# Loading the next chunk's activations in four parts, spread over two output products, in an attention and feed-forward kernel on one core

## The chip, the core and the metric

One core of one Trainium2 chip. The metric is the device time of one execution in microseconds (us). A kernel is run several times; a comparison uses runs of the two kernels on the same chip.

## The reference, cut to what matters

Hash attention is followed by a feed-forward block with a squared ReLU. The change lies in the second block:

```python
def _moe_ref(x, w_in, w_out):          # x: 3072 x 512, w_in: 512 x 2048, w_out: 2048 x 512
    h = x @ w_in
    r = np.maximum(h, 0.0)
    return ((r * r) @ w_out).astype(np.float32)
```

## The kernel before

Attention writes its result, transposed, to a buffer `x_all` in device memory. The feed-forward block then takes three chunks of 1,024 tokens. For each chunk it makes the hidden layer, and then the output in `project`, as seven output products (numbered 0 to 6) of a Strassen-like scheme. Each product is seven adds into PSUM. The chunk's x has a single buffer, so the next chunk's x is loaded while `project` runs, when x is no longer read.

In chunk 0 alone, `project` also prepares weights for the later chunks. At the start of each of products 0 to 3, `factor_units` loads two pieces of 256 KB ("h"), makes four sums of them on VectorE ("DVE" in the profiles), and stores pieces and sums. Loads of h, stores and loads of x all go through GpSimd's DMA queue. The stationary weights of each add ("leaf", 256 KB) are loaded through ScalarE's queue.

```python
    def load_x(i):
        x = p_c.tile([P, NFT, NCH], FP32, name="x")
        nc.gpsimd.dma_start(out=x, in_=x_all[:, :, i * NCH:(i + 1) * NCH])
        xs[i] = x, [p_c.tile([P, 2, NCH // 2], FP32, name=f"t_x{n}") for n in range(3)]

        def factor_units(n):
            src = [new_h()... for _ in range(2)]
            for j in range(2):
                nc.gpsimd.dma_start(out=src[j], in_=w_in_7[j * NQ + n, :, 5:7])
            sums = [new_h()... for _ in range(2)]
            sums_a(...)                                    # four sums on DVE
            for lo, hi, t in (...):
                nc.gpsimd.dma_start(out=w_in_49[n, :, :, lo:hi], in_=t)

        def product(n, w, at, bt, c11, c12, c21, c22, hook=None):
            ...
            add(0, at(0), bt["11"], True, False)
            one = keep(0, "one")
            add(1, at(1), bt["21"], True, True)
            if hook:
                hook()
            ...                                            # adds 3 to 6
            add(0, at(2), bt["t4"], False, True)           # the seventh reads what hook subtracted

            for k in range(7):
                ...
                if i == 0 and k < NQ:
                    factor_units(k)
                ...
                def hook():
                    y21 = b[:, NQ:NR, 0:QN]
                    minus(y21, y21, t2)
                    if k + 1 < 7 and k not in (1, 3):
                        inner_sums(k + 1)
                    ...
                product(NQ, QN, a_with_load, bt, ..., hook)
                if k == 0 and i + 1 < NCHUNK:
                    load_x(i + 1)
                if k in (3, 4) and i + 1 < NCHUNK:
                    sum_x(i + 1, 2 * k - 5)                # the first readers of the new x
                    sum_x(i + 1, 2 * k - 4)
```

On DVE the order within a product is: weight sums of `factor_units`, the hook's subtraction, inner sums of the next product, then sums of the outputs.

## Time and profile before

| | before |
|---|---|
| median of 3 runs | 880.21 us (880.0 to 881.27) |
| profiled run | 879.66 us, span 877.9 us |
| TensorE (PE) busy | 864.8 us |
| DVE busy | 760.4 us |
| TensorE idle in the output stage of chunk 0 (427 to 513 us) | 0.72 us |
| TensorE idle in the output stage of chunk 1 (605 to 692 us) | 0.00 us |

How to read it: one engine is busy for 98.5% of the span, so a change that moves no arithmetic is judged by the few places where that engine idles. The lines themselves are in the prediction below. In a timeline row the columns are start, duration, engine, source line, operation, output and input tiles, number of instructions, and in brackets the idle time just before, with what ended it ("issue": the profile shows nothing that the engine waited for).

### The profile page before, as it was taken

To read this page: it belongs to the slowest core of one execution; us is meant where nothing else is said; L and a number is where in the kernel's file an instruction comes from. 1 tells how busy PE (TensorE), PEld (TensorE's weight loads), DVE (VectorE), ACT (ScalarE), POOL (GpSimd) and SP (SyncE) were. 2 spreads that over 40 slices of the span, in tenths; PEclk is the share of its full clock that TensorE was granted. 3 is DMA by queue.
4 is the path that set the end of the run, shared out by engine and by line. 5 is a ranking of instruction groups with operands and counts; after the bars stand their busy time and mean duration, and the time that the engine had idled before them with its cause. 6 is when DMAs were issued, how large, how long until landed. Compare 5 with 4: busy or idle time off the path is not lost.

```text
span 877.9 us, 12130 instructions
## 1 busy us (share of the span) xinstructions
PE 864.8 (99%) x4340; PEld 518.7 (59%) x4340; DVE 760.4 (87%) x1099; ACT 391.5 (45%) x673; POOL 107.0 (12%) x172
## 2 busy tenths in 40 slices
PE   8999999999999999999999999999999999999996
PEld 3444444444444444444688865556888755568885
DVE  5999999999999998888779968888889788888875
ACT  6988888888888852222211123332111233321110
POOL 2000000000000001554231011111000211110002
PEclk9999999999999999999999999999999999999998
DMA  9777967998788536999897764536756754355565
GB/s 176 142 149 134 233 153 156 188 253 225 179 176 225 156 105 213 299 267 283 292 353 239 181 160 168 173 118 222 285 151 187 167 165 155 124 167 154 158 175 105
DMA packets 224131, 167.09 MB, mean 190 GB/s; under 512 B 164448, under 2 KB 181344, under 8 KB 224064
## 3 DMA queue, kind: packets, MB, share of 16 engines
q1 hardware_dynamic: 189152, 87.19, 41.0%
q0 software_dynamic: 12528, 41.30, 15.2%
q10 hardware_dynamic: 22384, 37.76, 14.0%
q8 instruction: 36, 0.59, 0.3%
q14 instruction: 31, 0.25, 0.1%
HBM read 124.52 MB, written 41.68 MB: 189 GB/s over the span
## 4 chain that ended last, share of the span: by engine, by line
PE 95%; DVE 2%; ACT 1%; DMA 1%; issue 0%; ACTq 0%; DVEq 0%
PE acc L712 40%; PE st L396 17%; PE acc L931 16%; PE xo L438 14%; PE acc L884 6%; PE hash L346 2%; PE tot L455 1%; DVE total L428 1%; DMA k_nat<-in_k_dram 1%; ACT bits L356 1%; ACT e L413 0%; PE xo L477 0%; DVE x_t L493 0%; PE tp L309 0%; DVE recs L487 0%
## 5 line engine op out<-in xcount | busy, mean ns | idle before, releaser
L413 ACT ACTIVATE e<-st 128x1024 f32<-128x1024 f32 x192 | 145.1, 810 | 44.9 <-PE st L396 41.0
L396 PE MATMUL st<-feat,feat 64*128 64x512 f32 (+1 forms) x768 | 150.4, 483 | 0.0
L438 PE MATMUL xo<-e,v_nat 128*64 128x512 f32 (+1 forms) x768 | 134.8, 492 | 0.0
L712 PE MATMUL acc<-b,leaf 128*128 128x256 f32 x600 | 133.2, 379 | 0.7 <-issue 0.7
L712 PEld LDWEIGHTS acc<-b,leaf 128*128 128x128 f32 x600 | 113.8, 190 | 17.1 <-issue 1.7
L428 DVE TENSOR_TENSOR total<-total,e 128x1536 f32<-128x1536 f32 x64 | 112.4, 1757 | 8.2 <-ACT e L413 3.6
L438 PEld LDWEIGHTS xo<-e,v_nat 128*64 128x64 f32 x768 | 51.3, 136 | 82.2 <-issue 74.3
L931 PE MATMUL acc<-t_x,w_unit 128*128 128x512 f32 x192 | 90.2, 592 | 0.0
L396 PEld LDWEIGHTS st<-feat,feat 64*128 64x128 f32 x768 | 66.0, 188 | 33.0 <-issue 23.2
L712 PE MATMUL acc<-t,leaf 128*128 128x256 f32 x336 | 76.3, 380 | 0.0
L356 ACT ACTIVATE bits<-hash,lifts 32x384 bf16<-32x384 f32 x120 | 68.6, 572 | 2.3 <-PE hash L346 0.5
L712 PEld LDWEIGHTS acc<-t,leaf 128*128 128x128 f32 x336 | 63.6, 190 | 9.4 <-DVE t L516 0.5
L796 DVE SCALAR_TENSOR_TENSOR b<-h 128x512 f32<-128x512 f32 x96 | 65.7, 691 | 3.0
L396 PE MATMUL st<-bits,bits 64*128 64x256 bf16 (+1 forms) x384 | 63.1, 325 | 1.7 <-ACT e L413 1.2
L931 PE MATMUL acc<-x,w_unit 128*128 128x512 f32 x128 | 60.1, 592 | 0.0
L712 PE MATMUL acc<-x,w_unit 128*128 128x512 f32 x128 | 56.6, 594 | 0.0
L712 PE MATMUL acc<-b_t,leaf 128*128 128x256 f32 x240 | 53.8, 379 | 0.0
L931 PEld LDWEIGHTS acc<-t_x,w_unit 128*128 128x128 f32 x192 | 36.5, 190 | 28.9 <-issue 26.8
L719 ACT COPY two<-acc 128x256 f32<-128x256 f32 (+1 forms) x29 | 12.5, 431 | 87.9 <-PE acc L712 63.1
L719 ACT COPY one<-acc 128x256 f32<-128x256 f32 (+1 forms) x29 | 12.5, 431 | 85.1 <-PE acc L712 46.9
L712 PEld LDWEIGHTS acc<-b_t,leaf 128*128 128x128 f32 x240 | 45.5, 190 | 6.2
L396 PEld LDWEIGHTS <-bits 64*128 64x128 bf16 x384 | 23.5, 93 | 42.5 <-issue 38.4
(159 smaller groups left out, 1165.5 us busy)
## 6 DMA issues: line engine op xcount, KB each, us to landing
leaf<-w_out ACTq DMA_DIRECT2D x142, 256.0 KB, 3.1
w_unit<-w_in SPq DMA_DIRECT2D x16, 640.0 KB, 4.0
raw<-in_moe_w_in_dram SPq DMA_DIRECT2D x16, 512.0 KB, 5.6
raw<-in_moe_w_out_dram SPq DMA_DIRECT2D x16, 512.0 KB, 4.6
w_unit<-w_in SPq DMA_DIRECT2D x8, 896.0 KB, 8.1
w_out<-sums POOLq DMA_DIRECT2D x16, 448.0 KB, 6.8
sum<-w_in SPq DMA_DIRECT2D x16, 448.0 KB, 4.8
v_nat<-in_v_dram SPq DMA_DIRECT2D x16, 384.0 KB, 4.3
```

The source lines that it names most:

```text
L346: nc.tensor.matmul(out=banks[g * NR_B:(g + 1) * NR_B, h, 0:HS], lhsT=projs[rows], rhs=feat[pr, w][rows, c * HS:(c + 1) * HS], start=True, ...
L356: nc.scalar.activation(out=t[h * D:h * D + NR_B, c * HS:(c + 1) * HS], in_=hashed[pr, w][at, h, 0:HS], func=ACTF.Sign, scale=HUGE, bias=li ...
L396: nc.tensor.matmul(out=st[:, h, 0:hi - lo], lhsT=src[pr, 1][rows, key], rhs=src[pr, 0][rows, lo:hi], start=first, stop=not first,)
L413: nc.scalar.activation(out=e[:, :, lo:hi], in_=sts[i][:, :, 0:hi - lo], func=ACTF.Exp, scale=scale)
L428: nc.vector.tensor_tensor(out=totals[pr], in0=totals[pr], in1=weights[pr, kt][:, :, 0:S], op=ALU.add)
L438: nc.tensor.matmul(out=xo[h * D:(h + 1) * D, lo:hi], lhsT=nat[pr, "v_nat"][:, h, kt * D:(kt + 1) * D], rhs=weights[pr, kt][:, h, lo:hi], s ...
L455: nc.tensor.matmul(out=tot[g * 32:(g + 1) * 32, 0:HS], lhsT=ones, rhs=totals[pr][:, h, c * HS:(c + 1) * HS], start=True, stop=True,)
L712: nc.tensor.matmul(out=acc[to], lhsT=a(i), rhs=b(i), start=first and i == 0, stop=last and i == n - 1, skip_group_check=True,)
L719: nc.scalar.copy(out=t, in_=acc[of])
L796: nc.vector.scalar_tensor_tensor(out=out, in0=h, scalar=0.0, in1=h, op0=ALU.max, op1=ALU.mult)
L884: nc.tensor.matmul(out=out, lhsT=w[:, a], rhs=b, start=start, stop=stop, skip_group_check=True)
L931: nc.tensor.matmul(out=acc[to], lhsT=w[:, PLACE[a], f], rhs=bt[b](f), start=first and f == 0, stop=last and f == NFT // 2 - 1, skip_group_ ...
```

## The change

Its intent is to thin out the burst of the 2,048 KB load: four parts of 512 KB, two during and after output product 0, two during and after product 1.

```diff
-    def load_x(i):
-        x = p_c.tile([P, NFT, NCH], FP32, name="x")
-        nc.gpsimd.dma_start(out=x, in_=x_all[:, :, i * NCH:(i + 1) * NCH])
-        xs[i] = x, [...]
+    def load_x(i, n=slice(0, NFT)):
+        if i not in xs:
+            x = p_c.tile([P, NFT, NCH], FP32, name="x")
+            xs[i] = x, [...]
+        nc.gpsimd.dma_start(out=xs[i][0][:, n], in_=x_all[:, n, i * NCH:(i + 1) * NCH])
...
                     minus(y21, y21, t2)
+                    if k < 2 and more:
+                        load_x(i + 1, slice(2 * k, 2 * k + 1))
...
-                if k == 0 and i + 1 < NCHUNK:
-                    load_x(i + 1)
+                if k < 2 and i + 1 < NCHUNK:
+                    load_x(i + 1, slice(2 * k + 1, 2 * k + 2))
```

More of the change, by code (lines that the diff above doesn't have):

```diff
@@ L549 @@
     xs = {}
-    def load_x(i):
-        x = p_c.tile([P, NFT, NCH], FP32, name="x")
-        nc.gpsimd.dma_start(out=x, in_=x_all[:, :, i * NCH:(i + 1) * NCH])
-        xs[i] = x, [p_c.tile([P, 2, NCH // 2], FP32, name=f"t_x{n}") for n in range(3)]
+    def load_x(i, n=slice(0, NFT)):
+        if i not in xs:
+            x = p_c.tile([P, NFT, NCH], FP32, name="x")
+            xs[i] = x, [p_c.tile([P, 2, NCH // 2], FP32, name=f"t_x{n}") for n in range(3)]
+        nc.gpsimd.dma_start(out=xs[i][0][:, n], in_=x_all[:, n, i * NCH:(i + 1) * NCH])
     w_unit = {}
```

## The prediction

> **What bounds the kernel now.** I read the page first: busy shares, then the chain that ended last.
>
> ```profile
> PE 864.8 (99%) x4340; PEld 518.7 (59%) x4340; DVE 760.4 (87%) x1099; ACT 391.5 (45%) x673; POOL 107.0 (12%) x172
> ...
> PE 95%; DVE 2%; ACT 1%; DMA 1%; issue 0%; ACTq 0%; DVEq 0%
> ```
>
> TensorE is busy for 864.8 of 877.9 us and carries 95% of the chain. The change moves no arithmetic, so it can gain only where TensorE stands still for the moved load, and lose only where the load newly makes it stand still. Next, busy time by stage. The load of the next chunk's x is issued in the output stage of chunk 0 (427 to 513 us) and of chunk 1 (605 to 692 us).
>
> ```profile
> 427.00:513.00 86.00, 85.28 (x393) 74.24 (x392) 79.26 (x123) 11.75 (x31) 19.34 (x30) 1.00 0.82 254
> ...
> 605.00:692.00 87.00, 87.00 (x400) 75.59 (x399) 78.66 (x116) 12.02 (x32) 8.05 (x13) 1.00 0.68 203
> ```
>
> Columns: stretch, its length, then busy us (and count) of PE, weight loads, DVE, ACT, POOL, then granted clock, DMA share, GB/s. TensorE loses 0.72 us in the first stage and nothing in the second. Thus the most that the change can win is 0.72 us, 0.08%. DVE is busy 79.26 of 86 us, so it has little room to be late.
>
> The timeline tells where the 0.72 us come from. First GpSimd's issues:
>
> ```profile
> 434.25 0.95 POOL L554 DMA_DIRECT2D x<-x_all  x1
> 435.01 1.28 POOL L837 DMA_DIRECT2D h<-w_in  x2
> 447.36 0.68 POOL L846 DMA_DIRECT2D w_in<-h  x1 [11.07 <-DMA h<-w_in]
> ```
>
> The 2,048 KB of x go out at 434.25 (11.9 us to landing, so 446.2), and the two 256 KB weight pieces h, issued right after, land only at 447.4 and 448.4: they queue behind x. Then all engines:
>
> ```profile
> 448.12 0.43 DVE L510 TENSOR_TENSOR h<-h 128x256 f32<-128x256 f32 x1 [1.21 <-DMA h<-w_in]
> ...
> 449.59 1.22 DVE L516 TENSOR_TENSOR b<-b,t 128x1024 f32<-128x1024 f32 x1
> ...
> 450.91 1.97 PE L712 MATMUL acc<-b,leaf 128*128 128x256 f32 x8 [0.72 <-issue]
> ...
> 456.54 0.42 DVE L510 TENSOR_TENSOR h<-h 128x256 f32<-128x256 f32 x1 [3.02 <-DMA h<-w_in]
> ...
> 473.41 1.22 DVE L516 TENSOR_TENSOR b<-b,t 128x1024 f32<-128x1024 f32 x1
> ```
>
> DVE waits 1.21 us for h, makes the four weight sums, then the subtraction of 449.59 that ends at 450.81. The seventh add of output product 1 reads that result and starts at 450.91, after 0.72 us of idling. The page labels the wait "issue"; I put it down to this subtraction, since the instruction order has TensorE wait for DVE there and the times fit. The last two rows are the same pair for product 2's weights and product 3's subtraction; they matter below.
>
> **What the Trainium skill says.** "DMA: Bandwidth & Descriptors", section "Queues, rings and completion order": each DMA engine consumes one queue's descriptors in ring order and round-robins between queues by packet. The trace agrees: h lands 1.2 us after x, and while x runs, the leaf weights of another queue take 7.1 to 7.9 us instead of the median 3.1. Section "Anatomy of one DMA — SWDGE (gpsimd) path": about 2.0 us plus bytes over 436 GB/s, so 512 KB alone would be an estimated 3.2 us and 2,048 KB 6.8 us; the trace has 11.9 us for the latter, because the DMA share is 0.97 to 1.04 from 436 to 452 us. The same section says that waits are held by the issuing sequencer and not by the DMA engines. "Perfetto Trace Analysis", section "Tensor Engine Instruction (MATMUL, LD_WEIGHTS)" has the elementwise engines as strict FIFO: the DVE wait for h delays everything after it, as the rows above show.
>
> **The change part by part.**
>
> (a) Count and bytes: two loads of 2,048 KB become eight of 512 KB, the same bytes and 4 KB rows. GpSimd gains six issues at an estimated 0.55 us (its 192 KB issues take 0.54), 3.3 us on an engine 12% busy: nothing on the path. DVE, TensorE and ScalarE keep their order.
>
> (b) Chunk 1 to 2. The order has no other GpSimd issue between the four parts, and all four stand where the old one stood, after the last peak loads (614.56 us). They go back to back and the stage keeps its zero idle: 0.0 us.
>
> (c) Chunk 0 to 1, first half. The order on GpSimd's queue becomes: stores of product 0's weight sums, x parts 0 and 1, h loads for product 1, its four stores, x parts 2 and 3, h loads for product 2. With x moving at (2,048 KB in 11.9 - 2.0 us) about 0.21 MB/us, 1 MB is 5 us: h for product 1 lands at an estimated 434.25 + 2 + 5 + 2 = 443.3 instead of 448.4. DVE reaches those sums at 446.9 (448.12 less 1.21) and no longer waits. The subtraction ends 1.2 us sooner, TensorE does not stop: **-0.72 us**, all of the idle.
>
> (d) Chunk 0 to 1, second half. Now x parts 2 and 3 stand before the h loads for product 2. DVE makes product 1's sums 1.2 us earlier, so the sum stores go out at about 448.2 instead of 449.5. From there the queue has 0.52 MB of stores, 1.05 of x and 0.52 of h. Before, the stores and h alone landed at 456.4, 7 us after 449.5. The extra 1.05 MB at some 0.25 MB/us (the queue moved 1.20 MB from 440 to 444 and 0.93 in the 4 us before) is 4.2 us; less the 1.3 us of earlier start, h lands near 456.5 + 2.9 = 459.4.
>
> What does it cost? DVE already waited 3.02 us for this h, until 456.54, and from there to the end of product 3's subtraction (473.41 + 1.22 = 474.63) is 18.1 us with only 0.25 us of idle. A late h moves that end almost one for one: 459.4 + 17.85 = 477.25. TensorE needs it for product 3's seventh add. A product lasts 12.09 us (452.71 to 464.80, starts of products 2 and 3), six of its seven adds 10.36, so it was due at 464.80 + 10.36 = 475.16, a margin of 0.5; with the 0.72 us of (c) it is due at 474.44. The stall: 477.25 + 0.1 - 474.44 = 2.9 us. Product 2's own subtraction ends at 459.4 + 2.7 = 462.1, against 462.35: just in time. Product 4's ended at 482.72 against 487.25 due, 4.5 us of room, so the delay stops there. **+2.9 us**.
>
> Sum: 880.21 - 0.72 + 2.9 = 882.4 us; I round to 882.3.
>
> **The rivals.** First, pure gain: if h for product 2 lands by 456.3, the halved burst costs nothing and only (c) counts: 879.5 us. For it: the parts are spread, and h's second load loses a 1.13 us wait for an earlier store. Against it: ring order, and a DMA share still 0.95 from 452 to 456. Second, no effect: gain and loss cancel (h near 457.1), 880.2 us. Third, leaf weights become the wait. In the old burst they landed as late as 8.4 us after issue (the one issued at 459.8), and they are asked for only five adds, 8.6 us, ahead. With x parts among stores and weights until 460 some could be late: another 0.5 to 2 us, 883 to 884.5. Fourth, x itself lands too late: its sums start at 479.10 and the last part should land near 458, so no.
>
> **Range and chances.** I hold the loss of (d) likelier than not, about 70%; pure gain or no effect 30%. The low end is the pure gain with run scatter, 879.2; the high end (d) with h 2 us later than I think, 884.6. To leave the 2% band takes 17.6 us, more than any chain here: same 0.98.
>
> **What would show it.** In the changed trace: (c) DVE runs product 1's sums without a wait near 447, and no idle near 450; (d) DVE waits past 456.5 for h, to about 459, and TensorE idles once for some 3 us near 474, before the seventh add of product 3; (b) zero idle in chunk 1's stage. I am wrong if h for product 2 lands before 457, if DVE has slack that I did not see between 459 and 474, or if TensorE waits for leaf.

## The result, and the profile after

The changed kernel took 883.40 us in the median of 6 runs (882.48 to 884.14), the kernel before 880.06 (6 runs, 879.69 to 881.27). The ratio is 1.0036, with a 95% interval of 1.0023 to 1.0049: slower by a third of a percent, and clear of noise. A ratio here is the mean time of one kernel's fast runs over that of the other's in the same rounds, so it is not quite the ratio of the medians quoted. At a threshold of 2% the two count as the same.

The page's busy line and then the busy time by stage of the changed kernel (columns as in the prediction):

```profile
PE 865.2 (98%) x4340; PEld 519.2 (59%) x4340; DVE 760.1 (86%) x1099; ACT 391.8 (44%) x673; POOL 109.8 (12%) x178
```

```profile
427.00:513.00 86.00, 82.65 (x380) 71.71 (x379) 76.66 (x116) 11.39 (x30) 20.09 (x32) 1.00 0.80 241
...
605.00:692.00 87.00, 87.00 (x397) 75.09 (x396) 77.25 (x111) 12.49 (x34) 9.40 (x16) 1.00 0.68 201
```

TensorE does the same work (865.2 us against 864.8) and idles 3.35 us in chunk 0's output stage, where it idled 0.72. Chunk 1's stage is untouched, at zero idle. The timeline of the changed kernel in chunk 0's stage, all engines (its source lines are up to 3 higher than before for the same code):

```profile
434.63 1.39 POOL L556 DMA_DIRECT2D x<-x_all  x2
...
447.20 0.42 DVE L510 TENSOR_TENSOR h<-h 128x256 f32<-128x256 f32 x1
...
449.71 1.39 POOL L556 DMA_DIRECT2D x<-x_all  x2
...
450.79 1.38 POOL L838 DMA_DIRECT2D h<-w_in  x2
...
460.49 0.43 DVE L510 TENSOR_TENSOR h<-h 128x256 f32<-128x256 f32 x1 [7.73 <-DMA h<-w_in]
...
461.96 1.22 DVE L516 TENSOR_TENSOR b_t<-b_t,t 128x1024 f32<-128x1024 f32 x1
...
463.27 1.97 PE L713 MATMUL acc<-b_t,leaf 128*128 128x256 f32 x8 [0.61 <-issue]
...
477.02 1.22 DVE L516 TENSOR_TENSOR b<-b,t 128x1024 f32<-128x1024 f32 x1
...
478.33 5.42 PE L713 MATMUL acc<-b,leaf 128*128 128x256 f32 x24 [2.74 <-issue]
```

DVE now starts product 1's weight sums at 447.20 without a wait, and TensorE has no idle near 450. That gain came. Ahead of product 2's h loads, however, two parts of x have been issued at 449.71. DVE waits 7.73 us for h, until 460.49. TensorE then idles before the seventh add of product 2 (0.61 us) and before that of product 3 (2.74 us), 1.3 us after the start of product 3's subtraction.

From the third add of product 0 to chunk 1's first matmul the trace before has 513.32 - 431.03 = 82.29 us, the trace after 516.40 - 431.42 = 84.98 us: 2.69 us more. The stage also began 0.39 us later in this trace, in a part of the program that the change doesn't touch; among all the traces below, that start scatters by 0.5 us. Together they are 3.08 of the 3.11 us between the two profiled runs (882.77 and 879.66).

### The profile page after: what moved, and what is told of

It is laid out like the page before. It is cut to its first block, busy times and chain, and to the rows that moved or that the text cites. A ratio compares the mean times of both kernels' runs of the same rounds, so it can differ in the third digit from the quotient of the medians.

```text
span 881.0 us, 12143 instructions
## 1 busy us (share of the span) xinstructions
PE 865.2 (98%) x4340; PEld 519.2 (59%) x4340; DVE 760.1 (86%) x1099; ACT 391.8 (44%) x673; POOL 109.8 (12%) x178
## 4 chain that ended last, share of the span: by engine, by line
PE 95%; DVE 2%; ACT 1%; DMA 1%; issue 1%; ACTq 0%; DVEq 0%
PE acc L713 40%; PE st L396 17%; PE acc L932 16%; PE xo L438 14%; PE acc L885 5%; PE hash L346 2%; PE tot L455 1%; DVE total L428 1%; DMA k_nat<-in_k_dram 1%; ACT bits L356 1%; ACT e L413 0%; PE xo L477 0%; DVE x_t L493 0%; PE tp L309 0%; DVE recs L487 0%
## 5 line engine op out<-in xcount | busy, mean ns | idle before, releaser
L438 PEld LDWEIGHTS xo<-e,v_nat 128*64 128x64 f32 x768 | 51.3, 136 | 82.1 <-issue 74.3
```

What stands on the lines that cost most here:

```text
L438: nc.tensor.matmul(out=xo[h * D:(h + 1) * D, lo:hi], lhsT=nat[pr, "v_nat"][:, h, kt * D:(kt + 1) * D], rhs=weights[pr, kt][:, h, lo:hi], s ...
```

## The experiments

The theory: what counts is who stands ahead of h on GpSimd's queue. A late h holds up DVE, which works in order, and DVE holds up the subtraction that TensorE's seventh add reads. The rivals: the number of DMAs, the DMA engines' bandwidth, or the leaf weights (on another queue). Each kernel gave correct results. Times are medians of 5 runs; the runs of the kernel before that they share have medians of 879.67, 879.71 and 879.72 us (9 runs in each). The short names follow the labels; the record has no run e7.

| kernel | time, us | ratio to before | DVE starts product 2's sums, us | TensorE idle in the stage, us |
|---|---|---|---|---|
| e1, whole load behind product 1's h | 879.05 | 0.9993 | 456.78 | 0.07, no row listed |
| e2, four parts in the old place | 879.93 | 1.0000 | 457.77 | 1.55 |
| e3, whole load ahead of product 2's h | 885.33 | 1.0064 | 463.25 | 3.62 + 2.74 |
| e4, h loads on SyncE's queue | 878.98 | 0.9993 | 452.41 | 0.00 |
| e5, all weight sums later on DVE | 880.10 | 0.9999 | 464.29 | 0.33 + 1.11 |
| e6, one part behind each h | 878.91 | 0.9988 | 456.18 | 0.00 |
| e8, second half behind product 2's h | 878.64 | 0.9984 | 456.64 | 0.00 |
| e9, change with filler matmuls | 882.76 | 1.0034 | 459.82 | 0.40 + 0.28, and 2.62 of filler |
| e10, only product 2's sums later | 878.58 | 0.9989 | 460.14 | 0.00 |
| the change, second series | 884.19 | 1.0045 | 460.15 | 0.32 + 2.74 |
| the change, third series | 884.32 | 1.0044 | 461.28 | 1.70 + 2.74 |

**e1: the load whole, but behind h.**

```diff
+        def factor_units(n, beside=None):     # beside() right after the two h loads
-                    factor_units(k)
+                    factor_units(k, (lambda: load_x(1)) if k == 1 else None)
-                if k == 0 and i + 1 < NCHUNK:
-                    load_x(i + 1)
+                if k == 0 and i == 1:
+                    load_x(2)
```

> Chunk 1's x stays one load of 2,048 KB, but is issued after product 1's two h loads instead of ahead of them. Theory (what matters is who stands ahead of h on GpSimd's queue, not the number of parts): h for product 1 lands near 439 us, DVE no longer waits for it, the 0.72 us of TensorE idle in chunk 0's output stage go away, and h for product 2 still lands by 456: about 0.7 us less than before, 879.3 us, with no splitting at all. Rival (splitting thins the burst, and the bandwidth of the burst is what hurts): one burst of the same size hurts as before, 880 us or more, idle of 0.7 us or more.

The time is 879.05 us. The busy time by stage of e1, and its DVE rows in the timeline:

```profile
427.00:513.00 86.00, 85.93 (x395) 74.61 (x394) 79.91 (x124) 11.75 (x31) 19.65 (x30) 1.00 0.82 254
```

```profile
446.85 0.42 DVE L510 TENSOR_TENSOR h<-h 128x256 f32<-128x256 f32 x1
...
456.78 0.43 DVE L510 TENSOR_TENSOR h<-h 128x256 f32<-128x256 f32 x1 [4.21 <-DMA h<-w_in]
```

Product 1's sums start without a wait, and the whole burst costs TensorE next to nothing. What the change set out to win comes without splitting. The ratio's interval, 0.9979 to 1.0007, does not exclude no change; the idle in the trace is the better witness for a gain of this size.

**e2: split, in the old place.**

```diff
                 if k == 0 and i + 1 < NCHUNK:
-                    load_x(i + 1)
+                    for n in range(4):
+                        load_x(i + 1, slice(n, n + 1))
```

> x in four parts, but all four back to back in the old place, after output product 0, for both chunks. Theory: six more issues on an idle engine, the same order of bytes: the same as before, 880.1 us within 0.4, TensorE idle in chunk 0's output stage 0.7 to 1.5 us (h waits up to some 1 us more for the extra issues). Rival (more DMAs, or their waits, are the cost): about the 883.4 us of the change.

The time is 879.93 us against 879.67, ratio 1.0000 (0.9986 to 1.0014). Its only idle in the stage is 1.55 us, in product 1, where before had 0.72: h is issued at 436.60, behind four issues of x, instead of 435.01. I had expected at most 1.5. The traced run is the slowest of the five, so the four issues may cost up to 0.8 us (1.55 less 0.72), which the medians do not show. The 3 us and more of the change they do not explain, nor do the parts for chunk 2: chunk 1's stage has zero idle here too.

**e3: a larger dose.**

```diff
-                if k == 0 and i + 1 < NCHUNK:
+                if k == 1 and i + 1 < NCHUNK:
                     load_x(i + 1)
```

> A larger dose: x as one load of 2,048 KB after output product 1, so twice the bytes of the change ahead of product 2's h loads, none ahead of product 1's. Theory: h for product 2 lands some 4.2 us later than in the change (460.4 there), near 464.5, and TensorE idles 4.2 us more than the 3.35 us of the change, 7 to 8 us in all, in product 2 (some 5) and product 3 (some 3): about 887.3 us. Rival (leaf weights or the extra DMAs are what TensorE waits for): no such growth, 881 to 884.5 us.

The direction and the mechanism came as expected, the size was smaller: 885.33 us, not 887.3. Two rows of e3's TensorE timeline:

```profile
466.04 1.97 PE L712 MATMUL acc<-b_t,leaf 128*128 128x256 f32 x8 [3.62 <-issue]
...
481.10 7.11 PE L712 MATMUL acc<-b,leaf 128*128 128x256 f32 x24 [2.74 <-issue]
```

With twice the bytes ahead of it, h let DVE begin at 463.25, 2.8 us later than in the change and not 4.2, and the idle grew by 3.0 us to 6.36. The idle before product 3's add stayed at exactly 2.74. The seventh adds of products 2 and 3 start 15.06 us apart (481.10 - 466.04), in the change too (478.33 - 463.27). That is the time that DVE needs from one subtraction to the next, while TensorE needs 12.09 for a product. Thus in these two orders, once TensorE has to wait for DVE in product 2 at all, the wait in product 3 is fixed, and only the one in product 2 grows with the lateness of h.

**e4: h on another queue.**

```diff
-                nc.gpsimd.dma_start(out=src[j], in_=w_in_7[j * NQ + n, :, 5:7])
+                queue = nc.gpsimd if n == 0 else nc.sync
+                queue.dma_start(out=src[j], in_=w_in_7[j * NQ + n, :, 5:7])
```

> The change as it is (four parts at its places), but the h loads of products 1 to 3 are issued by SyncE, so that they do not stand behind x on GpSimd's queue; the bytes and the time of the x parts are the same. Theory: h no longer comes after x, lands within some 8 us of issue, DVE is not held up past 456 us, TensorE idle in the stage goes to 0 to 0.3 us: about 879.4 us. Rival (the DMA engines' bandwidth is short, whatever the queue): h is late all the same or leaf is, and the time stays at 882 to 884.

The time is 878.98 us, with no TensorE idle in the stage. The x parts are issued within 0.3 us of their times in the change. This kernel is not clean, though: SyncE also issues h earlier, as soon as a buffer is free, since no stores stand before it. It shows that h need not be late while x is moved in four parts; it does not tell queue order from early issue (e8, below, comes closer).

**e5 and e10: the order on DVE.** In e5 the weight sums of all four products go behind the hook's subtraction and inner sums; in e10 only those of product 2.

```diff
                     minus(y21, y21, t2)
                     if k + 1 < 7 and k not in (1, 3):
                         inner_sums(k + 1)
+                    if (i, k) == (0, 2):              # e5: if i == 0 and k < NQ
+                        sum_units(k)                  # the four sums and their stores
```

In e5 the x part that the hook issues also comes behind these sums and stores.

> The change with all its loads in their order, but DVE makes product k's weight sums (the only readers of h on DVE) behind that product's subtraction and inner sums instead of ahead of them. h for product 2 lands as late as in the change, near 460. Theory (the stall is made by DVE's order: a late h holds up the subtraction that TensorE reads): DVE comes to the sums only near 460.4 and waits little, product 2's subtraction ends near 457, product 3's near 474, TensorE idle in the stage 0 to 0.3 us: 879.3 us. Rival (the idle labelled issue is a wait for leaf weights or for bandwidth, which this leaves untouched): 3 us of idle as in the change, 883 us.

e5 took 880.10 us, 0.8 more than expected. Its TensorE rows:

```profile
462.69 1.97 PE L713 MATMUL acc<-b_t,leaf 128*128 128x256 f32 x8 [0.33 <-DMA leaf<-w_out]
...
476.12 5.42 PE L713 MATMUL acc<-b,leaf 128*128 128x256 f32 x24 [1.11 <-issue]
```

Moving all the sums delayed product 0's stores too (437.87 instead of 433.50), and with them everything that follows on GpSimd's queue: h came nearly 4 us later than in the change. DVE waited 4.04 us for it even in the later place. Even so the idle fell from 3.35 to 1.44 us. The first row is the one place where the rival of the leaf weights shows: 0.33 us, with a leaf load that took 9.7 us to land. In the change none took over 7.5 us from 445 to 465. Since e5 moved more than it should, I made e10:

> The change with one move on DVE: only product 2's weight sums go behind product 2's subtraction and inner sums; all others and all loads stay, so h for product 2 lands near 460.3 as in the change. Theory (DVE's order carries the late h to TensorE): DVE comes to these sums near 460.4 and hardly waits, TensorE idle in the stage 0 to 0.3 us, 879.0 us. Rival (leaf or bandwidth): 3 us of idle, 883 us.

e10 took 878.58 us. Two of its DVE rows, then GpSimd's store of product 2's second piece (which waits for h to land), and its busy time in the stage:

```profile
455.31 1.23 DVE L516 TENSOR_TENSOR b_t<-b_t,t 128x1024 f32<-128x1024 f32 x1 [3.03 <-PE acc L713]
...
460.14 0.43 DVE L510 TENSOR_TENSOR h<-h 128x256 f32<-128x256 f32 x1
...
460.40 0.71 POOL L856 DMA_DIRECT2D w_in<-h  x1 [0.47 <-DMA h<-w_in]
```

```profile
427.00:513.00 86.00, 86.00 (x397) 75.16 (x396) 80.52 (x125) 11.75 (x31) 20.57 (x33) 1.00 0.82 254
```

All loads have the change's order, and DVE starts these sums at 460.14, as in the change (460.15 in its second trace). DVE was busy until 460.07, so that start alone does not date h; GpSimd's store does: 460.40, against 460.74 and 460.41 in the change's first two traces. So h was as late, but the subtraction had started at 455.31, and the 3.35 us of idle are gone. This settles the link that the label "issue" left open: TensorE waits for DVE's subtraction, which stood behind the late h. Bandwidth and leaf weights are as in the change, so they are not what TensorE waited for.

**e6 and e8: the parts behind h.** In e6 one part follows the h loads of each of products 0 to 3. e8 is the change with parts 2 and 3, as one load, behind product 2's h loads.

```diff
-                    factor_units(k)
+                    factor_units(k, lambda: load_x(1, slice(k, k + 1)))                    # e6
+                    factor_units(k, (lambda: load_x(1, slice(2, 4))) if k == 2 else None)  # e8
```

> Four parts of 512 KB, spread further: one behind the h loads of each of products 0 to 3, ahead of that product's stores. Theory: no part stands ahead of an h load that DVE is about to need, and each part has some 8 us to land; DVE's wait for product 2's h is at most the 3.0 us of before, no TensorE idle in the stage: 879.1 us, like the unsplit load behind h (879.05). Splitting adds nothing to that. Rival (thinner bursts are worth something of their own): below 878.7.

> Only the second half of the change altered: parts 0 and 1 as in the change, parts 2 and 3 as one load behind product 2's h loads instead of ahead of them. Theory: the gain of the first half stays (no wait of DVE near 447), the loss of the second half goes (h for product 2 by 456.5): 879.2 us, 4 us less than the change. Rival (the loss comes from the load lying in product 1 to 2 at all): 882 us or more.

They took 878.91 and 878.64 us, both with zero idle in the stage. In e8 the loss of the second half is gone and the gain of the first stays. It also speaks on why h was late: the bytes and the queue are the change's; x comes behind h, as one load of 1,024 KB, and h is issued 1.2 us sooner for it (449.59 instead of 450.79). From 450 to 460 us the DMA engines are as busy (share 0.99, in the change 0.97), yet DVE starts product 2's sums at 456.64, 3.85 us sooner and within 0.1 us of before (456.54). All its runs (878.20 to 878.96) lie below all 9 runs of before (879.37 to 880.87), ratio 0.9984 (0.9970 to 0.9998). e1, e4, e6, e8 and e10 lie within 0.5 us of each other, too close to rank.

**e9 and the change again: the rest of the time.** The change's 16 runs in three series spread from 882.10 to 885.03 us, those of e8 over 0.8 us. In its second trace the granted clock falls after the long idle. Busy time in two stretches right after it, first in the change's first trace, then in its second (the third number from the end is the granted clock), and between them the second trace's TensorE row:

```profile
478.00:480.00 2.00, 1.67 (x8) 1.52 (x9) 1.90 (x6) 0.00 (x0) 0.34 (x1) 1.00 0.82 290
480.00:482.00 2.00, 2.00 (x11) 1.77 (x10) 1.90 (x6) 0.00 (x0) 0.00 (x0) 1.00 0.00 0
```

```profile
478.00 6.92 PE L713 MATMUL acc<-b,leaf 128*128 128x256 f32 x24 [2.74 <-issue]
```

```profile
478.00:480.00 2.00, 2.00 (x5) 1.64 (x6) 1.86 (x6) 0.00 (x0) 0.00 (x1) 0.50 0.73 255
480.00:482.00 2.00, 2.00 (x9) 1.67 (x8) 1.93 (x5) 0.00 (x0) 0.00 (x0) 0.74 0.00 0
```

At a clock of 0.50 the view counts 5 matmul records in 2 us, where it counts 11 at full clock. The 24 records after the idle take 6.92 us instead of 5.42 in the first trace: 1.50 us. To test whether this is what separates the change's runs, e9 fills the idle:

```diff
             add(2, at(6), bt["22"], False, True)
+            if fill:                                   # 11 in product 3 of chunk 0
+                spare = ps_t.tile([P, 512], FP32, name="tp")[:, 0:P]
+                for _ in range(fill):
+                    nc.tensor.matmul(out=spare, lhsT=ident, rhs=ident, start=True, stop=True)
```

> The change, plus 11 matmuls of 128 x 128 of a constant (nobody reads the result) just ahead of the seventh add of product 3 in chunk 0, where TensorE stood idle for 2.74 us; they fill an estimated 2.4 us of that. Theory (beside the idle itself, the change loses some 1.5 us in those runs in which the granted clock falls to half after that idle, as in its second trace, and not in its first): no fall of the clock, all runs near the lower ones of the change, 882.5 us, within 0.8 us of each other. Rival (the change's runs differ because h lands at different times): median 883.3 or more, and runs 2 us apart, as in the change.

The change's third series ran beside e9, its second beside e5, e6 and e8. Their texts, the third first:

> The change itself, beside the two above. About 3.3 us of TensorE idle in two pieces; runs of 882.4 to 882.8 where the clock holds and of 883.4 to 884.5 where it falls to half for some 3 us after the longer piece; about 883.5 us in the median.

> The change itself once more, beside the same runs of before and on the same chip as these variants. Expected 883.3 us, 3.4 us of TensorE idle in two pieces, before the seventh adds of products 2 and 3. If h lands some 0.5 us later than in its first trace, both the idle and the time grow by about as much.

TensorE's rows in e9, then the stretch right after:

```profile
474.77 2.62 PE L739 MATMUL tp<-ident 128*128 128x128 f32 x22
477.67 5.42 PE L713 MATMUL acc<-b,leaf 128*128 128x256 f32 x24 [0.28 <-issue]
```

```profile
478.00:480.00 2.00, 2.00 (x11) 1.77 (x10) 1.90 (x6) 0.00 (x0) 0.00 (x0) 1.00 0.56 193
```

e9 loses as much as the change to the late subtraction (2.62 us of useless work stand where it idled), but its clock holds and its runs go from 882.13 to 883.06 us, 0.9 us apart (I had expected 0.8) where the change's third series is 2.9 apart. Its median is 1.56 us below that of the change on the same chip (882.76 and 884.32). Part of this may be an h that landed earlier: in the traced runs DVE starts product 2's sums at 459.82 in e9 and at 461.28 in the change's third series. The mean granted clock that is recorded for every run tells the two apart. Of the change's 16 runs the four at 0.997 took 882.10 to 882.77 us, the twelve at 0.995 or 0.996 took 883.40 to 885.03; all five of e9 are at 0.997 or 0.998. (A fall to half for 3 us would lower the mean by an estimated 1.5 of 881 us, 0.0017. The figure is coarse: three of e8's runs have 0.996 and no idle in the traced one.) So the half clock after the idle is a second cost of the change, of some 1.5 us in the runs that meet it. The lateness of h adds its own scatter. The change's third trace took 2.26 us more than the first (885.03 and 882.77): 1.09 are more idle before product 2's add, and 1.55 the clock (6.97 us for the 24 records), less 0.28 us of an earlier start of the stage, 2.36 in sum. My expectations for the change were low both times: 883.3 for 884.19 in the second series, 883.5 for 884.32 in the third. In the second I had tied a longer time to a later h; h came 0.3 us earlier in its trace, the idle was shorter (3.06 us), and the clock made up for it.

## Why the prediction was right, and where a term was off

- **What can be won, and the bound**: right. At most the 0.72 us of idle were to be won, and the kernels without it lie 0.6 to 1.1 us below before. Two of these exceed the bound (1.07 us in e8, 1.14 in e10), but their intervals hold 0.72, so no run shows the bound wrong.
- **(a) and (b)**: right. GpSimd issues two parts in 1.39 us and four in 2.10 us, and chunk 1's stage keeps zero idle in every trace; e2 confirms both.
- **(c), -0.72 us**: right. h for product 1 let the stores go at 444.5 and 445.6, later than the 443.3 estimated, yet ahead of DVE, which started at 447.20. e1 and e8 show the gain alone.
- **(d), +2.9 us in one piece**: right in mechanism, too small in size and wrong in shape. DVE started at 460.49 instead of 459.4; 0.4 us of this is the later start of the stage in that trace. The rest is the queue: from the sum stores (448.58) to DVE's start it took 11.9 us, where the prediction has 11.2 (448.2 to 459.4). I had product 2's subtraction "just in time" at 462.1 against 462.35. In fact TensorE already waited there, 0.61 us, and the wait in product 3 was then 2.74: 3.35 us in two pieces. The stage grew by 2.69 us where -0.72 + 2.9 = 2.2 was predicted.
- **What the sum lacked**: the fall of the clock after the idle, up to 1.5 us in some runs. The runs without it (882.10 to 882.77 us) lie around the 882.3 of the prediction; the medians, 883.40 to 884.32, lie above it.
- **The rivals**: pure gain and cancelling fell with h at 460. The leaf weights were not it (e10). The prediction misread one line there: the leaf load of 8.4 us, issued at 459.8, is not from x's burst, which had landed by 446.2. The x itself was not late: its first sums start at 482.70 without a wait.

Left open: what decides in which runs the clock falls. That h was late by its place in the queue, and not because the DMA engines had more to move, is what e8 shows; how the queue keeps that order no run takes apart. The words of the Trainium skill on ring order that the prediction cites stand in its paragraph on SyncE's and ScalarE's queues; for GpSimd's queue it is the landing times here that show the order.

## What to carry to other kernels

Before splitting a hidden load, ask what stands behind it on its queue, and when an engine will need that; here the place of the load was worth 3 to 6 us and the number of its parts nothing that the medians show. An in-order engine that waits early for something not urgent delays what is urgent behind it: moving four small sums behind a subtraction repaired the change as well as moving the load. And in this kernel, bound by TensorE, an idle of 2.74 us could cost half as much again (1.5 us) through the clock.

## What the Trainium skill lacked or had wrong

- "TensorE: Matmul & The Clock Gate", section "Part 1: The HAM clock gate (the "warmup" mystery)", ties the half clock to an idle window of about 3.4 us that runs freely, and its section "Why this matters for your kernels" asks for no gaps over about 3 us. Here idles of 2.74 us by the profile came before a clock of 0.50 in three of four traces (two of the change's three, and e3's), while e3's longer idle of 3.62 us was followed by full clock (1.00 from 466 to 468 us). So, as this profile counts idle time (it models where a matmul ends), 3 us is no safe limit, and a longer gap is no certain fall. The free-running window may explain both; no run here shows it.
- "DMA: Bandwidth & Descriptors", section "Anatomy of one DMA — SWDGE (gpsimd) path", gives a formula by size for each DMA. Two x parts of 512 KB, estimated from it at 3.2 us each, took 7.3 to 8.1 us behind stores at a DMA share of 0.93 (449 to 460 us), and the two 256 KB pieces of h behind them 8.7 and 9.1 us. The page has no figure for what a load costs those queued behind it.
- The section "Queues, rings and completion order" of that page says that the engines take turns between queues by packet, without saying how unequal this is. While x was moved (440 to 444 us in before), its queue took 74.3% of the engines' time for 292 packets (1.20 MB) and the leaf weights' queue 27.9% for 226 (0.42 MB), and a leaf load took over 7 us instead of 3.1. So the counts of packets are closer to each other than the bytes.
